# Loads that wait for the preceding TensorE operation of the order table, with the table made anew

## The chip, the cores and the metric

The kernel runs on one core of one Trainium2 chip. The metric is the device time of one launch in microseconds (us). The engines are TensorE (PE; its weight loads stand as PEld), VectorE (DVE), ScalarE (ACT), GpSimd (POOL) and SyncE (SP), whose queue issues every transfer of this kernel.

## The reference

Two independent problems, A and B, of the same shape: 16 batches of 80 rows, 32 query heads over 16 key/value heads, 512 cached keys, head width 128, all bf16. The two outputs are concatenated.

```python
def _A_ref(x, k_cache, v_cache, wq, wo):          # x (16,80,576), caches (16,16,512,128)
    q = transpose((x @ wq).reshape(B, Sq, Hq, Dh), 0, 2, 1, 3)
    k = jnp.repeat(k_cache, rep, axis=1)          # rep = 2 query heads to a key head
    v = jnp.repeat(v_cache, rep, axis=1)
    scores = jnp.einsum("bhqd,bhkd->bhqk", q, k) * (Dh ** -0.5)
    p = _softmax(scores, axis=-1)
    o = jnp.einsum("bhqk,bhkd->bhqd", p, v)
    return transpose(o, 0, 2, 1, 3).reshape(B, Sq, Hq * Dh) @ wo
...
return jnp.concatenate([a, b], axis=-1)
```

## The kernel before

The work is cut into 128 units (64 for each problem). A unit is one batch and four key heads, so 4 x 160 query rows: two heads of 80 rows share a key head. The 160 rows are handled as 128 + 32, and the four rests of 32 rows are put together to one tile of 128. So each unit has five score tiles of 128 x 512, numbered 5U to 5U+4, where 5U is the tile of the rests. For each unit and each group of eight units the operations are these; the short names are those of the code and of the text below.

- **ldk** (L631): one transposing load from the K cache for two units, so it is named by the even one (K8 is for units 8 and 9); **ldv** (L635): a plain load of V for one unit; **ldwa** and **ldwt** (L520, L524): pieces of wq; **ldwo** (L594): a quarter of wo; **ldx** and the like (L394, L450): x. K has buffers for six units, V for six.
- **xtr, xt** (L415, L433): TensorE transposes x at the start of problem A; POOL first copies a rest of x (L402).
- **qp, qt** (L551, L564): the q projection, four matmuls and one remainder per head and half; **qev** (L576 on ACT, L577 on DVE) moves q out of PSUM.
- **qk, qkr** (L678, L665): the scores; qkr does the rests of two units. **max** (L687, DVE), **exp** (L691, ACT), **rcp** (L697, DVE), **nrm** (L700, POOL) make the softmax.
- **tr** (L735): TensorE transposes the probabilities of two units, 80 small matmuls; **ptev, prev** (L752, L753, L761, L762) move them out on ACT or DVE.
- **pv** (L783): four matmuls for one key head; **oev** (L797) moves them out. Two units' pv follow their tr.
- **op** (L829): eight matmuls, half of one output tile of 128 x 288; **oea, oem, oeb** (L841, L851, L858) take it out on ACT or DVE, and **st** (L864) stores it from one of two buffers.

All operations are collected in `_Sched`. What order they run in is not worked out at run time: the string `ORDER` holds it, one letter for each operation (a stream of like operations, taken in turn), an apostrophe ahead of a letter for the other of two engines where an eviction may run on DVE or ACT, and a digit for each PSUM bank that the operation takes. `arrange` reads it. The result is one order of 5,242 operations over all engines; each engine runs its own of them in that order. `finalize` then derives the waits: an operation waits for the last writer of what it reads, and for the readers and the writer of what it overwrites, by semaphores, and leaves out a wait that an earlier one implies. A load therefore waits for nothing but the release of the buffer that it fills, and for its turn on SyncE's queue.

In the steady state a round of two units goes: tr of both, two qkr or one, then qk, pv, op and qp mixed until the next tr. The waits of PE on ACT and DVE inside a round are for banks that come free and for tiles that are moved out.

Of the kernel before, what the change touches and what calls it, by code (L numbers as in the profile page):

```python
# [8 lines left out]
AF = mybir.ActivationFunctionType  # L9
# [57 lines left out]
6425AmBh3'zg10z'yf7'xqf4f6'yf5pc2nacqc3mctc1c'uCpd2vnpc7vcm'tCb0pv'uCmwf4f3pbmvFipmvf1iCd5pmvif4d6ipmverg37w'A
Bmd0qveh5214nB'Ah0y'zf6x'yf3f2f5'zqc0acpCc4nvcd1p'uw'tc7pcmvf4tc0mcpf6b7'umCCpvpd3imvf2md0wpf5mvbpCmvd6rmveeBv
'Ag74'ABh1523qh0yn'zb6y'xqg15'zCCf7vnqbc2qwnpvf3ncpc1vmf4d0rvmpf5f6acpmd7Cpmvef4tc3mvcCpc2'Af5wumpvcd6'tf0Bd1'
uvpmieh2734AmiBih5'yzf6'xf1Cyf0v'zf2c3Cpcvc4tf7mcvpc5i'ud3vpmcwc6mtcb4Cpi'uvapmvf6f5pd1mwd2Cpmvf7bmpvmd0reeh64  # L70
75'A'BBh3'A'yg01x'zg62q'zc4'ycqc5nctc3i'ucCqnf0vf4c5qnb7tnwvpcf3pif6mbapmCf2vmb1Cpv'urmf0pd3vf5pmf4wd6Cpmvd7pm
bvmvd5rCCeevh1420A'A'BBh3z'yvwg56'xf7'yvqf4c2'zpcnc1cpf0'tif3qmc5b2unpf1mf7pcf6mCbtwpmvc5pmcd0vCipmf3avd4rmpd2
vud1mveeh3675A'B'BCh4'Avz'yg10vx'zf3J'yf2wCqc7cf6vpnc5f4pvcmb1p'tmqc7f3pmcbf2umnf6Cptc4wmcf5vd0iaCppmGd7vpmd3v
rmd2Cuveeh1546B'Aw'BCAh0v'y'zf3vb2p'xvy'zf7f4c5vmpcf0p'tf1ac3mpcc6mpbumCcwmf3Cf4pd0v'r'tc5pf2mvcd7pmvid1iumvJd
6ieeh3254A'A'BBh0y'zg16'yg23'xqb0qnqf5nbCqvnpc6vczc7'tcnf2uc4f1piGmcCpm'rvf3c6d7apf5vcmb2Cpw'utmvf1f0mpbvCpmvf
6d4mpvd1'rwd0miJeeh3652A'B'BCAh7'ywg04x'zvf1'zqf6c3'yvcqnf5c7tf2ncpc0if3'upcJmc4cab7mCppv'utmd1vpf0mf4Cbpvmpvf
5md6Cpvmd3Criwd0mveeCh7542'ABvw'ABh1y'zg06'zxvf3'yf5qf2vc7qcnvc1cnf4b0tpa'upmc7pf6mcpc1mcpd3f5mCtf2vbmpvCpmf4d
6vpmd5wCrmd7uveeh1024vA'B'ABvh6'zf7wx'yf3f5'yf0pc2ia'zcCpc6mvcf1uc4mcpc7'tcCpmf6wb2f3p'uvmpf7vd5'tpmvbiCpmivid
0mvd4'rmd6eeh7321A'B'BAh0y'zg56'xg43'zqc2qcnf1c7'ycCpb5vinCqvm'tc0ubwqnvf2rcnf1pvf6c5'tpcmf0f7pf4'uf3mb2pmCpvd
1md6wCpmpbvmCviad0rmvd5veeh3427'Aw'Ah1'BByv'zg56x'zf3'yf4qf2c7Ccqnvc1ctnf0vpc5ab7'upmpf6mbpmpcmf1f3Ctd2wmpc5vc  # L80
pCmf4id6vpmd0iFvCumd1rveeh4753Av'B'ABh2vy'zg61'xCqvf0'yf4c7'zvpcnf5f2wpc3a'tcpmc6cub7mqmc0cf4ptnf5pCbmvpmvf6d1
f2ipmiFd3Cpmvwd4rumvd5Cwveeh6702B'Av'Ah3'Byf1f5x'y'zb6'zCpvf7pmf4f2c3pmbvpmpcc0'rctmf1Cic7v'uf3apCcmd0vpmwf6c5
cmpd2vud4mvd5'teeh7163'B'BFh2'AAyFg40'z'yig57qb2'xqnqf1bnpCmc0zCwvcc6q'tf4cf1npvd0umc5vpcnf6vsb3aCpmvf4tmc2vpf
7cf1Cpmd5vpd6'uwmf4bvpmCimd7vseDiveCh4312B'A'ABvh5'yvwg76x'zf0'zqf4c1'ycqnc3f5tpf2ncc7ic'upc1amcpb6'utmpf3md0f
1Cpvmf4pvwmpbf7d5mCpKvmd3Csvd1mveeh4762'BBv'AAh5iD'yzg03K'xf7'zf4f1'yf6qCqc2vncpc5wncc0ticvmpb2DKp'umf7tpbmCmp
f4vd3pmvf5c1cmpwf0id7md6CpCsd4mvuDeveah1250A'BABvh7'yvCf3x'zf6f4v'zf1pc2'ycwpc0mcvpc7'ucp'tf3ac5mcpf0'ub2Ctmvp
mf5vbpmCd7msf1vd3mpid2vwimd0Deeh1465A'B'BAh3z'yg70'yxg24'zqc6f1cqc5nqcf3i'ub7pn'tCpvf5bmpwmqc1vcnf6td0mpc3d2sn
CCDevc'Biaf7mf4vpb5'uvCpmf2wd3'Apmf6vbpmvd0msvCeh4517vC'ABh2v'zf6x'yf0f5'yf3pvwc1a'zcpc2vmf4tcc7mpcc1'upcmb0tm
pf5Cf6'upf2vmbipwmipg14vmCd3qvmd6qvnd5nd2CCsveGeh7041B'Awv'BAh6vz'yg23'xf7'yqf5vf4'zc0qcnf6pc1nctc2icpmc3Dl0pD
mcab7pmLf5'uCuf0vmf4pbvpmd1f6Cpmvtd5mvpd0iwCsd3mwveeh2746'AAv'BCh1'Bvz'yf3f5x'zf7f2'ypf0vac6cpmc1ctc4mpcb6pmtc  # L90
3mcCpvf7'ubpmvDf1'uisf4md0pd3Cpmvd7md5wevKeh6214B'A'ABh0z'yg75'xg26'zqc1'yKqcnc4f3qic'tKc0Cnpf7wb1JnvJqubmvCpJ
nvcDf5mic2vpcf4'tb3smCpDw'uaf7mf0vpf1bvpmCf6pmd2vpd4mCsd5md7wviJeveh1360B'AvCBGh2'zAvg47x'yvf5'zqf3c6'ycqnf0c1
tf2cnpf6ac4'upcmc7tb1mppcmf4d3pmf0d5Cpvmd2uvmpf6biDwpmiCd4mvseevh6017AC'B'ABh3v'yCg25x'zwf4'yqvc1'zcpc3vncqf0v
ic6'ucl7tmDpf1nd4Lpmf2f7d5c3pmf0Cpmwetf1mvcpd6i'AvCB'uf7ad2pmvpemvh3540AmCh1yv'zf6f7CBv'xf3f5p'zf2wc4'ypcc0vmp
cc1vi'ucc6'ttcmpmud0b4pmf3Cf7mvpbpwmf5sd2vmpDd3iCmd1vaeveh4675A'B'ABh2'yg10x'zg34'yqc6'zcqnf7c2qc'tc5pinf1cb6p
mCtmvf0bpnvC'uf5wvf3maf7sqCf2d1npvc0pmb6vpmcvf5mud4Cpd3vpbmvFmwDd2siCeFevh5607A'B'BDCAvh4'zyg12'xyf5'zvwf3qc0c
vpc6nctf4i'uf7pc1macpb6mpmf0qf3bmpnCd5twmf7f1vc4Cppmcd2vpmd0vumd3svDeeh4176B'A'ABh2z'yg05'xCCvf1'z'yqf4c7vpcnf
3c2wpmcf6apvb0muvqf1mbpnd3mCpf4tc2vmpf5f7wcpmc1icvCsd6'tpmDvd4Cumd0veveh7251A'BAvh3'yzCvf6'yf4Bf2v'xb7pwpmf3c0
pamcbpmzf6mc4spc'tc2Cuf5cmvc0pf7'tcvd6Cp'uimvf3d2ipmwDid4id0mveeh3157B'ABh2y'zg60'xAg13'yqf4'zb5pnqf7mbpnqf6mf
4Cf2Csac0vncpc7vf5'tqCcmc1vpb0nvpmcvpf6bf3mtCwmupvid1mCwc4cd2pvmd5vid7'u'rCveeh4360B'B'AAwvh2'zg15vx'yf7'zqvf3  # L100
c6'ycqnf0c4pcnf2uc1ac'tpb5mpmf7tbpmpmf1c3Ccpmvf6f4d2Cpmvid7pmFvd0imwd1ruCveeh6453B'Av'BAh2y'zvg17'yxf6'zf4qc5f
2qcnf0c3pancb1p'umf7c3CpmtpbvmvCpf6f4mcvpc5mwricd2pmFvf7d1Cpmiwd0umvd6tCeveh7543A'B'BwAh2'zvf6x'yf1f5v'zf0pc4'
yf7pcmc3pcc2mictd6u'tmf1CCpf2vc3cpmvf5ib4p'uavmpbvmpCd3mvd0wm'rd1veeh4725A'B'ABh6z'yg30'xzg17'yqf2c5qcnf6b4p't
nCpvf3f5mqbvampc0ncc2CpC'ucc6'rc'twvvf0mud1pmf2f4b3qvmpwDinbCpivmf0vrd5mCpd6vd3mveevh2740A'B'BCAh1v'yzg53'xwzf
6'yb2vqqnf7c4pcnc5pmcf0tf3ic1'upcamf4tbmppf6mc1f5Cpd0mvf7Cpmcvd4pmwd3uimd6vrevGeh5127BC'A'Bh4vz'yg06'xvCAf5'yq
c1vc'zqc3wnf4cf7v'tiuc2nf0pf1af3pb6mpmcpc5mcCpf4wbmpvmuf7d0vmCpJd5vpmd3ivrmd1teeh7264A'B'ABCh5wv'zyf0'xf1pf3'y
# [37 lines left out]
class _Sched:  # L144
# [9 lines left out]
    def add(self, eng, key, emit, reads=(), writes=(), dsem=None, name="", stream=None, alloc=(), alt=None, hard=(), parts=()):  # L154
        op = _Op()
# [57 lines left out]
    def finalize(self):  # L213
# [7 lines left out]
        for op in ops:  # L221
            deps = {}
# [720 lines left out]
```

## Time and profile before

| | |
|---|---|
| median of 3 runs | 721.21 us (721.03 to 723.38) |
| profiled execution, its own time | 723.83 us |
| its span, first to last instruction | 722.1 us |
| granted TensorE clock, mean | 0.998 |
| PE, ACT, DVE, POOL busy | 98%, 90%, 85%, 60% |
| moved by DMA | 160.72 MB, mean 223 GB/s |

Shares of busy time are of the span. PE's matmuls are pipelined and their ends are modelled, so "busy" says that PE had work, not that it ran at its peak. "Idle before" is time in which an engine had nothing to do, put down to what ended the wait; "issue" is idle time with no wait that the profile shows. A load's line on SyncE is the time that its queue is held, and the landing is counted from the issue.

### The profile page before, as it was taken

How to read it: one execution, taken by the hardware profiler on the slowest of the kernel's cores; microseconds unless marked ns; L12 is line 12 of the kernel's file. 1: busy time of each engine (PE TensorE's matmuls, PEld its weight loads, DVE VectorE, ACT ScalarE, POOL GpSimd, SP SyncE). 2: the span in 40 equal slices, each digit the busy share in tenths (PEclk: the TensorE clock that was granted, in tenths of full speed). 3: DMA queues.
4: the chain of work that ended last, by engine and by line, in shares of the span. 5: the costliest groups of instructions: out<-in, count | busy, mean ns of one | idle time of the engine just before them, and what ended most of it. 6: DMA issues, size and time to landing. Idle time of an engine off the chain costs nothing.

```text
span 722.1 us, 26076 instructions
## 1 busy us (share of the span) xinstructions
PE 705.6 (98%) x10820; PEld 512.0 (71%) x10820; DVE 614.7 (85%) x1341; ACT 648.7 (90%) x1770; POOL 432.0 (60%) x650
## 2 busy tenths in 40 slices
PE   7898999999999999999999999899999999999998
PEld 4565677777777767767677777677777777777777
DVE  2997989889788888888989888698898988889994
ACT  2998989999999999989999999799999999999893
POOL 0566656666666564755766576455665656566663
PEclk9999999999999999999999999999999999999999
DMA  9999997999879999999999899789799889979390
GB/s 238 247 271 264 269 254 178 245 254 238 218 195 231 268 220 226 262 226 229 258 226 238 229 211 267 180 212 217 149 296 231 209 230 222 254 178 211 101 225 23
DMA packets 374166, 160.72 MB, mean 223 GB/s; under 512 B 278560, under 2 KB 370976, under 8 KB 374048
## 3 DMA queue, kind: packets, MB, share of 16 engines
q1 hardware_dynamic: 374048, 159.05, 92.2%
q8 instruction: 86, 1.41, 0.8%
q14 instruction: 32, 0.26, 0.1%
HBM read 87.65 MB, written 2.95 MB: 125 GB/s over the span
## 4 chain that ended last, share of the span: by engine, by line
PE 90%; SPq 4%; DVE 3%; DMA 1%; issue 1%; ACT 0%
PE ps L829 22%; PE ps L783 19%; PE ps L551 17%; PE ps L678 15%; PE ps L735 11%; PE ps L665 4%; PE ps L564 3%; SPq L631 2%; DVE negmax L687 2%; DMA v_sb<-in_A_v_cache_dram 1%; SPq L520 1%; DMA out_dram<-osb 1%; SPq L394 0%; SPq L524 0%; ACT p_sb L691 0%
## 5 line engine op out<-in xcount | busy, mean ns | idle before, releaser
L700 POOL TENSOR_SCALAR p_sb<-p_sb,rinv 128x512 bf16<-128x512 bf16 x640 | 430.2, 692 | 272.6 <-DVE rinv L697 272.2
L691 ACT ACTIVATE p_sb<-ps,negmax 128x512 bf16<-128x512 f32 x640 | 438.0, 711 | 19.1 <-DVE negmax L687 16.9
L687 DVE TENSOR_REDUCE negmax<-ps 128x1 f32<-128x512 f32 x640 | 410.1, 678 | 20.7 <-PE ps L678 12.3
L783 PE MATMUL ps<-pT,v_sb 128*128 128x160 bf16 x2048 | 181.5, 233 | 2.8 <-issue 2.2
L829 PE MATMUL ps<-wo_sb,oT 128*128 128x288 bf16 x1280 | 181.6, 287 | 2.2 <-issue 2.2
L783 PEld LDWEIGHTS ps<-pT,v_sb 128*128 128x128 bf16 x2048 | 152.7, 98 | 42.3 <-ACT pT L752 5.2
L678 PE MATMUL ps<-kT,qT 128*128 128x512 bf16 x512 | 166.4, 381 | 2.6 <-DVE rinv L697 1.1
L551 PE MATMUL ps<-xT,wq_sb 128*128 128x320 bf16 x1024 | 163.5, 299 | 0.9 <-DMA wq_sb<-in_A_wq_dram 0.6
L829 PEld LDWEIGHTS ps<-wo_sb,oT 128*128 128x128 bf16 x1280 | 123.4, 98 | 44.5 <-issue 2.9
L691 ACT ACTIVATION_READ_ACCUMULATOR p_sb<-ps,negmax 128x1 f32 x640 | 145.1, 227 | 0.0
L551 PEld LDWEIGHTS ps<-xT,wq_sb 128*128 128x128 bf16 x1024 | 97.5, 98 | 43.8 <-issue 1.3
L752 ACT COPY pT<-ps 128x512 f32<-128x512 f32 x194 | 105.0, 603 | 8.7 <-PE ps L735 6.7
L577 DVE TENSOR_SCALAR qT<-ps 128x320 bf16<-128x320 f32 x125 | 57.0, 483 | 41.9 <-PE ps L564 41.7
L735 PEld LDWEIGHTS ps<-ident,p_sb 64*128 64x128 bf16 x5120 | 82.6, 95 | 9.6 <-ACT p_sb L691 1.7
L735 PE MATMUL ps<-ident,p_sb 64*128 64x64 bf16 x5120 | 86.1, 190 | 0.9 <-ACT qT L576 0.3
L576 ACT ACTIVATE qT<-ps 128x320 bf16<-128x320 f32 x131 | 50.9, 437 | 28.5 <-PE ps L564 27.8
L797 DVE CAST oT<-ps 128x320 bf16<-128x320 f32 x138 | 65.6, 479 | 9.0 <-PE ps L783 8.6
L678 PEld LDWEIGHTS ps<-kT,qT 128*128 128x128 bf16 x512 | 45.4, 98 | 31.7 <-DVE pT L753 4.4
L797 ACT CAST oT<-ps 128x320 bf16<-128x320 f32 x118 | 51.7, 444 | 9.9 <-PE ps L783 9.1
L753 DVE COPY pT<-ps 128x1024 bf16<-128x1024 bf16 x62 | 42.0, 682 | 3.7 <-PE ps L735 3.6
L697 DVE RECIPROCAL rinv<-rowsum 128x3 f32<-128x3 f32 (+1 forms) x256 | 39.6, 159 | 5.4 <-ACT p_sb L691 4.6
L665 PE MATMUL ps<-kT,qT 128*32 128x512 bf16 x512 | 37.4, 383 | 1.3 <-issue 1.3
(31 smaller groups left out, 147.7 us busy)
## 6 DMA issues: line engine op xcount, KB each, us to landing
v_sb<-in_A_v_cache_dram SPq DMA_DIRECT2D x64, 512.0 KB, 5.0
v_sb<-in_B_v_cache_dram SPq DMA_DIRECT2D x64, 512.0 KB, 5.2
wo_sb<-in_A_wo_dram SPq DMA_DIRECT2D x8, 576.0 KB, 6.5
wo_sb<-in_B_wo_dram SPq DMA_DIRECT2D x8, 576.0 KB, 6.2
wq_sb<-in_B_wq_dram SPq DMA_DIRECT2D x4, 1024.0 KB, 6.9
out_dram<-osb SPq DMA_DIRECT2D x40, 72.0 KB, 3.9
wq_sb<-in_A_wq_dram SPq DMA_DIRECT2D x8, 256.0 KB, 4.4
wq_sb<-in_A_wq_dram SPq DMA_DIRECT2D x2, 1024.0 KB, 7.1
```

What stands on the lines that cost most here:

```text
L551: last = e.matmul(ps[:, vbq[h].phys, QO:QO + 320], lhsT=wq_sb[:, wsl, ck, hi * 128:(hi + 1) * 128], rhs=xT[:, half, ck, n0:n0 + 320], star ...
L577: return e.tensor_scalar(dst, src, SCALE, None, op0=AluOpType.mult)
L665: last = e.matmul(ps[32 * g4:32 * g4 + 32, vb_.phys, :], lhsT=qT[:, qsl_, bl_, g4 * 160 + 128:g4 * 160 + 160], rhs=k_of(U_, g4), start=Tru ...
L678: return e.matmul(ps[:, vb.phys, :], lhsT=qT[:, qsl, bl, gl * 160:gl * 160 + 128], rhs=k_of(U, gl), start=True, stop=True)
L687: return e.tensor_reduce(negmax[:, si:si + 1], ps[:, vb.phys, :], axis=AX.X, op=AluOpType.max, negate=True)
L691: return e.activation(p_sb[:, psl, :], ps[:, vb.phys, :], AF.Exp, bias=negmax[:, si:si + 1], scale=1.0, accum_out=rowsum[:, ss, k:k + 1])
L700: return e.tensor_scalar(p_sb[:, psl, :], p_sb[:, psl, :], rinv[:, ss, k:k + 1], 1.0, op0=AluOpType.mult, op1=AluOpType.mult)
L735: last = e.matmul(dst, lhsT=p_sb[64 * h:64 * h + 64, psl2[i_][k_], j * 128:(j + 1) * 128], rhs=ident[64 * h:64 * h + 64, 64 * h:64 * h + 6 ...
L752: return e.copy(dst.bitcast(F32), ps[:, vb.phys, :].rearrange("p (j n) -> p j n", j=4))
L783: last = e.matmul(ps[:, vo.phys, off:off + 160], lhsT=v_sb[:, vs, gl, j * 128:(j + 1) * 128], rhs=pT[:, pts, j, :, 32 * gl:32 * gl + 32], ...
L797: return (e.copy if en == "act" else e.tensor_copy)(dst, src)
L829: last = e.matmul(ps[:, vb.phys, 0:DC], lhsT=oT[:, sp_ * (HH // 2) + i, rb * 128:(rb + 1) * 128], rhs=wo_sb[:, 2 * c3 + sp_, i, :], start= ...
```

## The change

In `finalize`, operations are gone through in the table's order. The last TensorE operation seen is remembered, and each operation whose name begins with "ld" (all 248 loads, not the 40 stores) gets it as a further dependency. So a load is issued no earlier than the end of the TensorE operation that stands ahead of it in the table. Waits implied by an earlier one on the same queue are left out as before: of SyncE's operations 186 now carry a wait for PE, 140 did before.

```diff
 class _Op:
     __slots__ = ("eng", "key", "seq", "emit", "reads", "writes", "dsem", "stream", "alloc", "alt",
-                 "deps", "signals", "sidx", "waits", "clock", "name", "hard", "parts")
+                 "deps", "signals", "sidx", "waits", "clock", "name", "hard", "parts", "paced")
...
         op.parts = list(parts)
+        op.paced = name.startswith("ld")
...
         cur_ver = {}
+        last_pe = None
         for op in ops:
...
             for d in op.hard:
                 deps[id(d)] = d
+            if op.eng == "pe":
+                last_pe = op
+            elif op.paced and last_pe is not None:
+                deps[id(last_pe)] = last_pe
...
 ORDER = """
-oEHoj7KHKHIIHNk6Hk0NMl1Hk4LMIMEIl5d6ad3k4k0eL'BMMd4Ad1d3eId7B'AId0d2aed5'A'Bd4d1eA'Bd3e'ABe'AK'BKf0f3ipf6f1af5
...
+HKIHHHIKIoEj2oNNHHIk6ak4k0l5EMLMMd1d0d2el7d3Iek4d6I'Bd5ALBMed4Kd0aKied3'A'B'B'Ad7k2d1ed5eMBA'A'A'Bf0pg3iaf5f4d
...
```

The table is new from its first letter to its last. What differs once it is decoded:

- PE has the same 1,842 operations. The round's frame (tr, qkr, qk, pv, op and qp of the same numbers between two tr) is the same; inside a round neighbours change places.
- Four evictions move from ACT to DVE (1,129 operations become 1,125, and 1,337 become 1,341). Which of the evictions run where, and their places, change throughout.
- SyncE's first loads. Before: wq 0.0, x 0.0, wt 0.0, x 0.1, wt 0.1, wq 1.0, wt 1.0, wq 0.1, 0.2, 0.3, wt 1.1, wq 1.1, K0, wq 1.2, 1.3, K2, x 1.0, x 1.1, V0, K4, V1, V2, K6, V3. After: wq 0.0, x 0.0, wq 1.0, wt 0.0, wt 0.1, wq 0.1, wt 1.0, x 0.1, wt 1.1, wq 0.2 (waits for the warm-up matmuls), wq 0.3, wq 1.1, K0 (xtr0), wq 1.2 (qp0.1.1), wq 1.3, x 1.0 (qp0.3.0), K2 (qp0.3.1), x 1.1, V0, V1 (qkr0), K4, V2 (qk6), V3 (tr1), K6.
- From there on nearly every load stands behind a later PE operation than the release of its buffer. Two examples, as PE's order runs from the operation waited for to the first reader. K8: qk33, then pv3.2 pv3.3 tr4 qk34 tr5 qkr7 qk36 op pv4.0 pv4.1 qk37 qk38 pv4.2 pv4.3 qp1.6.0 pv5.0 qk39 pv5.1 pv5.2 op pv5.3, then qk41. V127: pv125.2, then pv125.3 op op tr126 tr127 op pv126.0 to pv126.3, then pv127.0.

More of the change, by code (lines that the diff above doesn't have):

```diff
@@ L67 @@
[L67 to L106, printed above, removed]
@@ L128 @@
+c2cf7c3cf6c5cf0bc4tppCpsm'umf7if3cig62pqpCqm'u'tmnDb1bf0vvvvwvwvvvh4675mnh3'zpsCyf2'zf1f6f4b5pxmymCppmc7cDc0cc
+3cbm'tuCpmc0ic'utsCb6vwvvvvwvvvbh0271h5b3'xsyz'zyc0cDc6cc1Dcc5bt'tuscb7'ubb3sDDbsD
 """
```

88 lines of the change are left out of this document (63 added, 25 removed).

## The prediction

> **What bounds the kernel now.** I read the page first: busy shares, then the chain that ended last.
>
> ```profile
> PE 705.6 (98%) x10820; PEld 512.0 (71%) x10820; DVE 614.7 (85%) x1341; ACT 648.7 (90%) x1770; POOL 432.0 (60%) x650
> PE 90%; SPq 4%; DVE 3%; DMA 1%; issue 1%; ACT 0%
> ```
>
> TensorE is busy 98% of the span and is 90% of the chain, so a change that leaves its matmuls as they are can save at most the rest, 722.1 - 705.6 = 16.5 us. Where that rest lies is in the windows by stage (busy time of each engine, granted clock, DMA share, GB/s):
>
> ```profile
> 0.00:40.00 40.00, 33.98 (x348) 19.35 (x350) 25.85 (x60) 25.68 (x70) 15.33 (x30) 1.00 1.06 243
> 40.00:100.00 60.00, 56.29 (x917) 39.69 (x909) 52.92 (x113) 54.46 (x149) 36.32 (x55) 1.00 1.15 262
> 100.00:300.00 200.00, 199.24 (x3072) 146.23 (x3070) 173.17 (x375) 188.65 (x520) 124.19 (x185) 1.00 0.97 230
> 450.00:458.00 8.00, 5.79 (x128) 3.88 (x126) 5.17 (x10) 7.22 (x20) 3.96 (x6) 1.00 0.77 187
> 458.00:461.40 3.40, 3.40 (x15) 1.89 (x14) 1.43 (x4) 0.34 (x2) 1.26 (x2) 0.50 0.09 20
> 600.00:722.00 122.00, 119.53 (x1868) 90.03 (x1864) 102.69 (x223) 104.19 (x284) 71.80 (x107) 1.00 0.70 168
> ```
>
> PE idles 6.0 us in the first 40 us, 3.7 us in the next 60, 0.8 us in the 200 after that, 2.2 us in the 8 us from 450, and 2.5 us in the last 122, most of it the end. From 458.0 to 461.4 the granted clock was 0.50, straight after the stop at 455, which costs half of 3.4, 1.7 us, without being idle. So the game is in the start and in a few single stops; the middle runs without gaps. PE's waits say who ends them (total, times, longest):
>
> ```profile
> PE ps L829 <- issue: 2.2, 1, 2.2
> PE ps L783 <- issue: 2.2, 4, 1.4
> PE ps L415 <- DMA acc<-in_A_x_dram: 1.3, 2, 0.7
> PE ps L665 <- issue: 1.3, 1, 1.3
> PE ps L433 <- POOL acc L402: 0.6, 1, 0.6
> PE ps L783 <- DMA v_sb<-in_A_v_cache_dram: 0.6, 1, 0.6
> PE ps L551 <- DMA wq_sb<-in_A_wq_dram: 0.6, 1, 0.6
> ```
>
> Two kinds. Waits for a load come to 1.3 + 0.6 + 0.6, and the 0.6 for POOL's copy of x is one more, all in the first 40 us. The others, "issue", ended without any semaphore; the three long ones are 1.4, 1.3 and 2.2 us. The timeline shows two of them, one inside a run of equal matmuls, where the order of instructions asks for no wait:
>
> ```profile
> 53.02 0.85 PE L783 MATMUL ps<-pT,v_sb 128*128 128x160 bf16 x10
> 55.25 0.30 PE L783 MATMUL ps<-pT,v_sb 128*128 128x160 bf16 x2 [1.37 <-issue]
> 457.47 1.35 PE L829 MATMUL ps<-wo_sb,oT 128*128 128x288 bf16 x7 [2.21 <-issue]
> ```
>
> **What a load costs, and what the new wait does to it.** SyncE's line of loads (duration on its queue, ns) and the time from issue to landing, first for K (L631), then for V (L635):
>
> ```profile
> L631 SPq DMA_TRANSPOSE kT<-in_A_k_cache_dram x32: 3894/5556/9213, 8.6 to 331.3; - x32
> DMA to landing us min/median/max: 6.1/8.1/12.9
> DMA to landing us min/median/max: 3.8/5.0/9.4
> ```
>
> A K load holds SyncE's queue for 5.6 us and lands 8.1 us after its issue; a V load lands after 5.0 us. Everything behind a waiting load on that queue waits too: later loads, and the output stores. In exchange the queue is now idle where it used to run ahead as far as free buffers allowed.
>
> The unit costs of PE's operations, to turn an order into time, stand in the chain (start, us, what):
>
> ```profile
> 59.17 1.09 PE ps L551 x8
> 81.18 0.98 PE ps L829 x8
> 95.56 1.17 PE ps L735 x80
> 152.71 1.11 PE ps L783 x16
> 236.03 1.02 PE ps L665 x16
> 314.51 1.19 PE ps L678 x5
> ```
>
> So one qp is 1.09/2 = 0.55, one op 0.98, the transposes of a pair 1.17, one pv 1.11/4 = 0.28, one qkr of two units 0.51, one qk 0.24 us. The lead of a load is PE's work between the end of the operation that it now waits for and the first operation that reads it. For K8 (wait for qk33, read by qk41) that is 10 pv, a pair of transposes, one qkr, 5 qk, 2 op and one qp: 2.8 + 1.2 + 0.5 + 1.2 + 2.0 + 0.55 = 8.2 us. Counted so for all 64 K loads, the median lead falls from 19 us (from the last wait that the old order gave) to 14, and the shortest, beyond the first two loads, are 8.2, 8.4, 8.8, 9.2, 9.4, 9.4, 9.9, 10.3 and 10.3 us. For the 128 V loads the median falls from 30 to 17 us; five lie below 7: 5.6, 6.0, 6.0, 6.1 and 6.8 (V127, the first of these: 5 pv, 3 op and a pair of transposes, 1.4 + 2.9 + 1.2).
>
> **Term 1, the start: -1.7 us.** The first loads change places. Timeline of before:
>
> ```profile
> 1.24 3.27 PE L367 MATMUL ps<-wo_sb 128*128 128x512 bf16 x8 [1.24 <-DVE wo_sb L360]
> 2.60 0.60 SPq L394 DMA_DIRECT2D acc<-in_A_x_dram  x1
> 5.17 1.71 SPq L520 DMA_DIRECT2D wq_sb<-in_A_wq_dram  x3
> 9.63 1.79 PE L551 MATMUL ps<-xT,wq_sb 128*128 128x320 bf16 x12 [0.56 <-DMA wq_sb<-in_A_wq_dram]
> 15.30 4.86 SPq L631 DMA_TRANSPOSE kT<-in_A_k_cache_dram  x1
> 20.21 2.06 SPq L394 DMA_DIRECT2D acc<-in_A_x_dram  x2
> 22.82 6.90 SPq L631 DMA_TRANSPOSE kT<-in_A_k_cache_dram  x1
> 24.98 0.38 PE L415 MATMUL ps<-ident,acc 128*128 128x128 bf16 x4 [0.61 <-DMA acc<-in_A_x_dram]
> 25.20 0.59 PE L678 MATMUL ps<-kT,qT 128*128 128x512 bf16 x2
> ```
>
> ```profile
> acc<-in_A_x_dram SPq DMA_DIRECT2D x2, 288.0 KB, 3.8
> ```
>
> The second half of x (part 1.0) stood behind K2 and made PE wait 0.61 us at 24.98; it now goes ahead of it, and the wait is gone. V1 stood behind K4 and cost 0.6; it now goes ahead of it, gone. In the first 10 us wq piece 0.1 moves from 8th to 6th place, which lifts the 0.56 at 9.63, while x part 0.1 moves from 4th to 8th: issued at 5.2 instead of 2.6, it lands 3.8 later, near 9 us, and its wait (0.6 before) stays about what it was. The new waits cost nothing here: the 10th load waits for the warm-up matmuls, over at 1.24 + 3.27 = 4.5 us, when SyncE has issued only about six. Together -0.6 - 0.6 - 0.5. What is late next: K2 is issued half a microsecond later, 15.8, lands near 15.8 + 8.1 = 23.9, and is needed at 25.20 less what was gained; so at most 1.3 us of the gain gets past that point at once. Bounds: 0 (all is taken by the next wait) and -2.5 (the 0.6 for POOL goes too).
>
> **Term 2, the stops without a semaphore: -1.3 us.** Stops of 1.4 and 1.3 us fall in the stage of the highest DMA share (1.15), where the old queue ran furthest ahead. In the new order that stage's loads are spread: K8 waits for qk33, K10 for qk42. I take one of the two as gone, as an estimate from that coincidence only; bounds 0 and -2.7, and a new stop elsewhere (+2.2, with the half clock +3.9) can't be excluded. [...]
>
> **Term 3, loads that come late: +0.6 us.** Leads of 8.2 and 8.4 us meet a K landing after 8.1: a few tenths each for K8 and K10, nothing for the rest. The cover is PE's own work between; where a K takes longer than its lead, PE stands for the difference, since nothing else may pass in its queue. Bounds: 0 with K at its minimum of 6.1, and with K at 10.5 (half way from median to maximum) the shortfalls of the nine leads above sum to 2.3 + 2.1 + 1.7 + 1.3 + 1.1 + 1.1 + 0.6 + 0.2 + 0.2 = 10.6 us. V at 5.0 is covered everywhere; at 7 us the five short ones would cost 4.5.
>
> **Parts at nothing.**
>
> ```profile
> L797 ACT CAST oT<-ps 128x320 bf16<-128x320 f32 x118 | 51.7, 444 | 9.9 <-PE ps L783 9.1
> ```
>
> The matmuls are the same in number and shape, and nearly the same in order. Four evictions move from ScalarE (94% busy in 100 to 300 us) to VectorE (87%), 4 x 0.44 = 1.8 us of work off the fuller engine, hidden behind PE on either. PE's additional signals for SyncE are part of matmuls that run anyway. Each output store keeps over 5 us of PE work between its latest wait and the eviction that needs its buffer. Bounds of the remade middle are under the second rival.
>
> **Sum.** The profiled execution took 723.8 us, span 722.1; the runs' median, 721.2, is 2.6 lower. The stop at 455 with its half clock is 2.2 + 1.7 = 3.9, so I take 2.6 of it as this execution's own. 723.8 - 2.6 - 1.7 - 1.3 + 0.6 = **718.8 us**. A measurement of this kernel tells about 0.3%, 2.2 us, from no change: "faster" is below 719.0, "slower" above 723.4.
>
> **Rivals.** (a) *Late K loads decide.* The new wait replaces a free-running queue by leads of 8 to 10 us. It decides once a paced K needs over 9.4 us from its wait to its landing. For it: landings up to 12.9 us. Against: the long ones come with a backlog, and pacing removes backlog. Price: the 10.6 us above instead of 0.6, 728.8. Chance 0.17.
> (b) *The remade middle is looser.* 64 rounds of two units, each with its orders on ScalarE and VectorE changed; a tenth of a microsecond lost per round is 6.4 us, 725.2. For it: ScalarE is 94% busy there, so an eviction placed a little late has little to hide in. Against: the order differs by neighbours, and the old one lost 0.8 us in 200. Chance 0.14.
> (c) *Loads were never on PE's path after the start, and the stops stay.* Term 2 falls out: 720.1, no measurable change; the same if terms 1 and 3 cancel. [...] Chance 0.24.
> (d) *Both early stops, and further small waits, go*: the calmer DMA also lets VectorE and ScalarE start on time in 40 to 100 us, where PE idles 3.7 us. 718.8 less 1.3 and less 2.5 of those: 715. Chance 0.10.
> Forecast: 0.35, spread 717 to 721, so some of it falls in the band.
>
> **How the numbers follow.** Faster: 0.10 from (d), 0.28 of the forecast, 0.04 of (c): 0.42. Slower: (a) and (b), 0.31. Same: the rest, 0.27. The range reaches from 713.5 (a little below (d)) to 728.8, the price of (a), which leaves out less than 2 in 10. The likeliest case's own range is 716 to 722.
>
> **What would show it.** Right: no wait of L415 for x at about 24 us and none of L783 for V1; PE idle in 0 to 100 us near 7 instead of 9.7 us; at most one stop of over 1 us without a releaser before 100 us; PE over 99% busy in 100 to 300 us; median K landing below 8.1. Wrong by (a): PE waiting for kT at L678 or L665, at qk41, qk51, qkr111. Wrong by (b): waits for DVE or ACT spread evenly over the middle, with VectorE waiting for PE more than before.

## The result, and the profile after

The changed kernel takes 717.62 us (median of 8 runs, 715.94 to 721.89), the kernel before beside it 721.59 us (8 runs, 721.03 to 724.85): a ratio of 0.9944, 95% interval 0.9919 to 0.9970. (Ratios leave disturbed runs out, so they are not exactly the quotients of the medians.) The profiled execution took 720.19 us with a span of 718.3, 3.8 us below the 722.1 of before. Lines are 6 higher than before: qk is L684, pv L789, op L835, qp L557, qkr L671, ldk L637, ldv L641.

The page's busy shares and the chain by engine:

```profile
PE 704.7 (98%) x10820; PEld 511.7 (71%) x10820; DVE 617.8 (86%) x1345; ACT 647.4 (90%) x1766; POOL 431.9 (60%) x650
PE 89%; DMA 7%; DVE 1%; SPq 1%; issue 1%; ACT 0%; POOL 0%
```

PE's idle time fell from 16.5 to 718.3 - 704.7 = 13.6 us. DMA, 1% of the old chain, is 7% of the new one: loads are now issued late enough to be followed back into. The windows by stage, after (start:end, length, then busy us of PE, PEld, DVE, ACT and POOL with their counts, granted clock, DMA share, GB/s):

```profile
0.00:40.00 40.00, 33.48 (x326) 19.05 (x326) 24.96 (x58) 25.05 (x67) 14.20 (x29) 1.00 1.04 235
40.00:100.00 60.00, 59.32 (x949) 41.65 (x950) 55.60 (x120) 57.39 (x160) 39.32 (x59) 1.00 1.10 257
100.00:300.00 200.00, 198.86 (x3073) 145.47 (x3073) 174.00 (x377) 187.26 (x512) 123.09 (x183) 1.00 0.99 228
300.00:450.00 150.00, 148.17 (x2322) 108.36 (x2315) 132.49 (x292) 139.10 (x379) 93.41 (x140) 1.00 0.99 228
450.00:600.00 150.00, 149.69 (x2343) 109.97 (x2341) 130.87 (x285) 140.26 (x384) 91.28 (x136) 1.00 0.97 229
600.00:718.30 118.30, 115.14 (x1826) 87.17 (x1825) 99.87 (x219) 98.33 (x268) 70.61 (x105) 1.00 0.76 185
```

and the two stages of before that the prediction did not show:

```profile
300.00:450.00 150.00, 149.03 (x2333) 108.97 (x2331) 134.02 (x297) 139.42 (x381) 92.93 (x140) 1.00 0.97 238
450.00:600.00 150.00, 147.52 (x2308) 107.74 (x2305) 126.08 (x276) 136.30 (x372) 91.46 (x137) 0.99 0.91 220
```

PE's idle time, stage by stage, before and after: 6.0 and 6.5; 3.7 and 0.7; 0.8 and 1.1; 1.0 and 1.8; 2.5 and 0.3; 2.6 and 3.2 (from 600 to the end of the span). Two stages gained, 3.0 and 2.2 us, and the second of them also lost its half clock (1.7 us of busy time). The other four lost 0.5, 0.4, 0.9 and 0.6 us, 2.3 in all (from unrounded rows). The two that gained are those that held the long stops without a semaphore. (The trace of the changed kernel holds no clock records, so its 1.00 are no readings; that PE had no half clock there is told from its matmuls: after the first 4 us and apart from the stops, five output matmuls in a row start at most 125 ns apart (122 in the median; 240 in the half clock of before), five of the projections at most 175 (136 in the median). The second profile of this kernel, below, has records, and they say 1.00 from 5.4 us on.) Of PE's waits after (total, times, longest):

```profile
PE ps L557 <- issue: 1.3, 2, 0.8
PE ps L557 <- DVE xT L426: 1.1, 1, 1.1
PE ps L684 <- DMA kT<-in_A_k_cache_dram: 1.0, 1, 1.0
PE ps L789 <- issue: 1.0, 1, 1.0
PE ps L421 <- DMA acc<-in_A_x_dram: 0.7, 2, 0.5
PE ps L671 <- DVE rinv L703: 0.6, 1, 0.6
PE ps L671 <- DMA kT<-in_B_k_cache_dram: 0.3, 1, 0.3
PE ps L671 <- DMA kT<-in_A_k_cache_dram: 0.2, 1, 0.2
```

The wait for V1 is gone, and the one for x at 25 us nearly. A K wait of 1.0 us stands in their place, and two more waits of the start are new: 1.1 us for VectorE's copy of x, ahead of the first projections (now at 7.05 instead of 9.63 us), and 0.6 us for rcp at 22.96. The timeline shows the K wait at K2's first reader:

```profile
26.49 0.59 PE L684 MATMUL ps<-kT,qT 128*128 128x512 bf16 x2 [1.04 <-DMA kT<-in_A_k_cache_dram]
```

K2 was issued at 16.59 and landed at 26.35, 9.8 us later; in the kernel before it was issued at 15.30 and landed 8.3 us later. Over all K loads the landing (min/median/max) is not shorter than the 6.1/8.1/12.9 of before:

```profile
DMA to landing us min/median/max: 6.1/8.7/12.7
```

### The profile page after: what moved, and what is told of

Read it like the earlier page. It is cut to its first block, busy times and chain, and to the rows that moved or that the text cites. A ratio compares the mean times of both kernels' runs of the same rounds, so it can differ in the third digit from the quotient of the medians.

```text
span 718.3 us, 26080 instructions
## 1 busy us (share of the span) xinstructions
PE 704.7 (98%) x10820; PEld 511.7 (71%) x10820; DVE 617.8 (86%) x1345; ACT 647.4 (90%) x1766; POOL 431.9 (60%) x650
## 4 chain that ended last, share of the span: by engine, by line
PE 89%; DMA 7%; DVE 1%; SPq 1%; issue 1%; ACT 0%; POOL 0%
PE ps L835 21%; PE ps L789 18%; PE ps L557 18%; PE ps L684 15%; PE ps L741 10%; PE ps L671 4%; PE ps L570 3%; DMA kT<-in_A_k_cache_dram 3%; DMA kT<-in_B_k_cache_dram 2%; DVE negmax L693 1%; DMA xst<-in_B_x_dram 1%; DMA acc<-in_A_x_dram 1%; DMA wq_sb<-in_A_wq_dram 1%; DMA out_dram<-osb 1%; ACT p_sb L697 0%
## 5 line engine op out<-in xcount | busy, mean ns | idle before, releaser
L789 PE MATMUL ps<-pT,v_sb 128*128 128x160 bf16 x2048 | 182.1, 233 | 1.0 <-issue 1.0
L789 PEld LDWEIGHTS ps<-pT,v_sb 128*128 128x128 bf16 x2048 | 152.8, 98 | 37.9 <-DVE pT L768 4.9
L835 PE MATMUL ps<-wo_sb,oT 128*128 128x288 bf16 x1280 | 179.8, 286 | 0.0
L684 PE MATMUL ps<-kT,qT 128*128 128x512 bf16 x512 | 167.5, 380 | 2.4 <-DMA kT<-in_A_k_cache_dram 1.0
L557 PE MATMUL ps<-xT,wq_sb 128*128 128x320 bf16 x1024 | 165.4, 299 | 2.8 <-issue 1.3
L835 PEld LDWEIGHTS ps<-wo_sb,oT 128*128 128x128 bf16 x1280 | 123.2, 98 | 40.8 <-ACT pT L758 0.6
L557 PEld LDWEIGHTS ps<-xT,wq_sb 128*128 128x128 bf16 x1024 | 97.9, 98 | 46.8 <-issue 2.5
L758 ACT COPY pT<-ps 128x512 f32<-128x512 f32 x190 | 103.4, 603 | 7.1 <-PE ps L741 5.2
L583 DVE TENSOR_SCALAR qT<-ps 128x320 bf16<-128x320 f32 x124 | 56.5, 484 | 37.5 <-PE ps L570 37.4
L684 PEld LDWEIGHTS ps<-kT,qT 128*128 128x128 bf16 x512 | 45.1, 97 | 31.8 <-ACT pT L758 8.3
L803 ACT CAST oT<-ps 128x320 bf16<-128x320 f32 x116 | 50.0, 442 | 5.0 <-PE ps L789 4.6
L759 DVE COPY pT<-ps 128x1024 bf16<-128x1024 bf16 x66 | 44.4, 683 | 4.7 <-PE ps L741 4.6
L671 PE MATMUL ps<-kT,qT 128*32 128x512 bf16 x512 | 37.6, 383 | 1.5 <-DVE rinv L703 0.6
```

The source lines that it names most:

```text
L557: last = e.matmul(ps[:, vbq[h].phys, QO:QO + 320], lhsT=wq_sb[:, wsl, ck, hi * 128:(hi + 1) * 128], rhs=xT[:, half, ck, n0:n0 + 320], star ...
L583: return e.tensor_scalar(dst, src, SCALE, None, op0=AluOpType.mult)
L671: last = e.matmul(ps[32 * g4:32 * g4 + 32, vb_.phys, :], lhsT=qT[:, qsl_, bl_, g4 * 160 + 128:g4 * 160 + 160], rhs=k_of(U_, g4), start=Tru ...
L684: return e.matmul(ps[:, vb.phys, :], lhsT=qT[:, qsl, bl, gl * 160:gl * 160 + 128], rhs=k_of(U, gl), start=True, stop=True)
L758: return e.copy(dst.bitcast(F32), ps[:, vb.phys, :].rearrange("p (j n) -> p j n", j=4))
L789: last = e.matmul(ps[:, vo.phys, off:off + 160], lhsT=v_sb[:, vs, gl, j * 128:(j + 1) * 128], rhs=pT[:, pts, j, :, 32 * gl:32 * gl + 32], ...
```

## A count that explains the stops

The stops without a semaphore have a place in common that no view names, but that the views can count. The page of before says:

```profile
q8 instruction: 86, 1.41, 0.8%
```

Queue q8 brought 86 packets of instructions, 1.41 MB, each of 16,384 bytes in the trace. PE's stream has 10,820 matmuls, as many weight loads and 340 semaphore and drain instructions in the trace: 21,980, or 256 for each packet. Read by this count, the queue brought PE's instructions in blocks of 256, one for every 126 matmuls or so, on average every 705.6 / 86 = 8.2 us of PE's busy time. The windows from 0 to the end of the four long stops of before count the matmuls ahead of it (the bracket behind PE's time):

```profile
0.00:55.24 55.24, 47.85 (x595) 29.25 (x596) 39.78 (x89) 40.66 (x111) 24.69 (x44) 1.00 1.08 255
0.00:63.27 63.27, 54.60 (x721) 33.89 (x721) 45.88 (x102) 47.36 (x128) 28.79 (x50) 1.00 1.09 250
0.00:90.93 90.93, 81.20 (x1098) 52.26 (x1099) 70.44 (x154) 72.47 (x199) 45.66 (x76) 1.00 1.11 258
0.00:457.46 457.46, 443.79 (x6771) 317.68 (x6772) 391.13 (x852) 414.89 (x1134) 272.26 (x413) 1.00 1.00 238
```

With weight loads and semaphore instructions these are instructions 1216, 1473, 2240 and 13,760 of the stream: 192, 193, 192 and 192 beyond a multiple of 256. (The count starts at the first instruction of the profile; what PE ran ahead of it is not counted. The place 192 to 194 is called a block boundary from here on.) The stop at 90.9 is put down to DVE by the waits, but sits at the same place. And the stop at 55.25, which began at 53.88, has a packet of q8 right ahead of it (DMA queues, 52.8 to 54.0 us):

```profile
q8 instruction: 1, 0.02, 5.4%
```

In the trace that packet ran from 52.85 to 53.89, and PE went on 1.36 us after its end. For the other three the pause from the packet's end to PE's restart is 1.23, 1.63 and 1.28 us. This suggests a theory that the first four runs were not chosen for: these stops are PE waiting for a block of its own instructions that comes late (theory F below).

## The experiments

The experiments ran on three chips, four to a chip, each time with the kernel before beside them: there its medians were 723.49, 723.21 and 723.46 us, and on the last chip its 33 executions ranged from 717.04 to 727.91 us. The ratios are to these.

**First four: which half of the change does it?** Three theories were on record: P, the wait gives the gain; T, the new table gives it; M, the calmer middle pays.

Table only:

```diff
-            elif op.paced and last_pe is not None:
+            elif False and op.paced and last_pe is not None:
```

> The new table without the new wait. Theory P (the wait gives the gain: with the queue held back, PE's stops without a semaphore between 40 and 100 us do not happen): the two stops of over 1 us come back, about 720 to 721.5, ratio to before 0.997 to 1.000. Rival T (the new table gives the gain, by the order of the first loads and of the evictions): as the changed kernel, 717.6, ratio 0.994, no stop of over 1 us before 100 us.

Measured: 721.11 us, ratio 0.9973 (0.9948 to 0.9998). The early stops are gone without the wait, which is against P; but others stand at 217 us (0.8 us, at matmul 3115, where the changed kernel stopped too), 258, 513 and 521 us. The last is put down to ACT, but it too sits at a block boundary:

```profile
PE ps L789 <- ACT p_sb L697: 1.3, 1, 1.3
PE ps L557 <- issue: 1.2, 2, 0.9
PE ps L789 <- issue: 1.1, 2, 0.8
PE ps L671 <- issue: 0.8, 1, 0.8
```

Wait only, that is the changed code with the old string:

```diff
 ORDER = """
-... (the new table)
+... (the old table)
 """
```

> The old table with the new wait. Theory P: the stops before 100 us go, 718 to 719, ratio about 0.996; no wait for kT, since the old table's loads stand early in it. Rival T: the old time, 721.6, or slower by late loads.

Measured: 731.83 us, ratio 1.0106 (1.0068 to 1.0143). PE's waits:

```profile
PE ps L421 <- DMA acc<-in_A_x_dram: 3.4, 1, 3.4
PE ps L835 <- issue: 2.8, 1, 2.8
PE ps L557 <- DVE osb L864: 2.2, 1, 2.2
PE ps L557 <- DMA wq_sb<-in_B_wq_dram: 1.0, 1, 1.0
PE ps L671 <- issue: 1.0, 1, 1.0
```

The first x load stands behind the warm-up matmuls in the old table, so now it waits for them, and PE starts on x at 8.3 instead of 5.2 us; the projections behind this wait ran at half pace (the first eight in 2.34 us, 1.25 at full pace). A store that stands behind a paced load in SyncE's queue is late and costs 2.2 us, a late wq piece 1.0. Stops came back at matmuls 721, 1098 and 6771 of before (1.0, 0.8 and 2.8 us), at other times and with the queue held back. So P's account of them falls: neither a queue that runs ahead nor its absence decides.

Wait in the first 103 us alone, and wait in the rest alone, both with the new table:

```diff
-            elif op.paced and last_pe is not None:
+            elif op.paced and last_pe is not None and op.key < 714:     # the start
+            elif op.paced and last_pe is not None and op.key >= 714:    # the other kernel: the rest
```

> The new table, loads wait for PE only up to about 103 us, later ones only for their buffers. Theory P: as the changed kernel within a microsecond, 717 to 718.5, since the stops lie in the start. Rival T: 717.6 too; a third, M (the calmer DMA of the middle pays): 720 or more.

Measured: 720.73 us, ratio 0.9958 (0.9931 to 0.9986).

> The new table, loads wait for PE only from about 103 us on. Theory P: as without the wait, 720 to 721.5, with stops in 40 to 100 us. Rival T: 717.6. M: 718 or less.

Measured: 717.31 us, ratio 0.9903 (0.9872 to 0.9934). By these numbers M seemed to hold: pacing the middle worth some 4 us on top of the table. But the profiles differ in PE's stops at block boundaries: counting those of 0.3 us or more, 4.1 us in all in the table-only kernel, 2.8 with the start paced, 1.1 with the rest paced. The next runs test whether that is all.

**The changed kernel again, on another chip.**

> The changed kernel unaltered, so that the next ones have it on the same chip. Theory F (a PE stop that no wait explains is PE waiting for its own instructions: a block of 256 instructions comes in as one 16 KB packet of the instruction queue, and the packet is late) expects the ratio to stay near 0.994 and, in the profiled run, zero to two stops of 0.7 us or more after 40 us, every one of them at PE instruction 192 to 194 of a block of 256, not necessarily at the places of the first profile of this kernel. Rival R (a stop belongs to a place in the program: to what the operation there does or reads) expects the stop at the same operation again, the third output matmul of the 36th V unit at 219 us, 1.0 us.

Measured: 717.90 us, ratio 0.9915 (0.9885 to 0.9946). Its stops came at matmuls 2611 (0.8 us), 7651 (0.4) and 7778 (1.0), all at 192 to 194 of a block, while the first profile of the same kernel had them at 1099, 3115 and 4627. A further 0.7 at matmul 5137 is a wait for x's transposes in problem B, which the waits name and which has no packet near it; so "every one" in the expectation of F was too much, and R's stop at 219 us did not come. Two of the first profile's three, 0.5 and 0.8 us there, came back at 0.2 us each (1099 and 4627). So the length of a stop changed from one execution to the other; where in the block PE stopped, at 192 to 194, did not.

**The kernel before, shifted by 30 instructions.**

```diff
-            for _ in range(NWARM):
+            for _ in range(5):
                 last = e.matmul(ps[:, vw.phys, :], lhsT=ones, rhs=warm, start=True, stop=True)
+            for _ in range(18):
+                last = e.matmul(ps[:, vw.phys, 0:64], lhsT=ones, rhs=warm[:, 0, 0:64], start=True, stop=True)
```

> The kernel before with 23 warm-up matmuls in place of 8 (5 of 512 columns and 18 of 64, together a little shorter), which shifts everything later in PE's instruction stream by 30 instructions and leaves table, loads and waits as they were. The kernel before had stops at matmuls 595, 721, 1098 and 6771 counted from the first (instructions 1216, 1473, 2240 and 13760), and the run with the old table and the wait had them again at 721, 1098 and 6771. F expects those that come back at the same counts, which are now operations 15 matmuls earlier in the program, or none at all where a block boundary now lies in a slower stretch; none at the old operations, which now stand at matmuls 610, 736, 1113 and 6786. R expects them at the old operations, so at matmuls 610, 736, 1113 and 6786. Time: F and R both within 3 us of the kernel before (718.5 to 724.5); F alone allows a difference from which blocks are late.

Measured: 718.06 us, ratio 0.9920 (0.9887 to 0.9953). The old table without any new wait, with 15 more warm-up matmuls, gains as much as the whole change. Its windows:

```profile
0.00:40.00 40.00, 35.61 (x359) 21.11 (x361) 25.67 (x60) 25.15 (x70) 14.94 (x30) 1.00 1.09 236
40.00:100.00 60.00, 59.21 (x944) 41.90 (x940) 55.60 (x120) 57.08 (x159) 39.83 (x60) 1.00 1.13 266
100.00:300.00 200.00, 200.00 (x3150) 146.67 (x3149) 173.22 (x376) 189.51 (x521) 125.47 (x187) 1.00 1.02 237
300.00:450.00 150.00, 147.19 (x2236) 108.13 (x2233) 130.85 (x290) 136.85 (x374) 90.77 (x136) 0.99 1.01 231
450.00:600.00 150.00, 149.98 (x2351) 110.46 (x2349) 131.35 (x287) 140.70 (x384) 92.82 (x138) 1.00 0.95 223
```

From 40 to 100 us PE idles 0.8 us instead of 3.7, and 450 to 600 is full. Matmul by matmul against the kernel before: at 34.8 us the two are level to 0.02 us, so the warm-up's new form gave nothing; the shifted one is ahead by 1.4 us at the old place of the stop at 55, by 1.9 at that at 63, 3.2 at that at 91, 3.7 at a shorter one at 220, falls back by 3.1 at its own one long stop and the half clock behind it, and gains 4.1 over the old stop and half clock of 457. At the end it is 5.2 ahead. The time is 0.4 us below what either theory had room for. The old first stop lay inside this run of pv, which now has none (timeline):

```profile
53.15 0.99 PE L785 MATMUL ps<-pT,v_sb 128*128 128x160 bf16 x12
...
347.58 1.09 PE L785 MATMUL ps<-pT,v_sb 128*128 128x160 bf16 x7 [2.32 <-issue]
```

The one at 347.58 stands ahead of matmul 5133, instruction 10,432, again 192 of a block. The wait-only kernel, and the old table with the wait on the rest (two runs further down), have stops of 1.5 and 1.7 us ahead of matmul 5133 too (the kernel before one of 0.4), there a matmul of qp, here one of pv 15 matmuls earlier in the program. A count shared by three kernels, at two different operations: windows from 0 of the wait-only kernel, of the old table with the rest paced, and of this one,

```profile
0.00:355.66 355.66, 343.80 (x5133) 243.97 (x5133) 298.14 (x647) 316.54 (x867) 207.62 (x315) 1.00 1.01 236
```

```profile
0.00:354.02 354.02, 341.30 (x5133) 242.43 (x5133) 297.81 (x647) 316.73 (x867) 207.67 (x315) 1.00 1.04 237
```

```profile
0.00:347.57 347.57, 339.60 (x5133) 242.52 (x5134) 295.52 (x643) 315.68 (x866) 207.61 (x315) 1.00 1.05 240
```

F's places hold and R's do not: nothing stopped at matmuls 610, 736, 1113 or 6786. The only other stop over 0.7 us after 40 us, 0.8 at 56.5, is a K load that came late, which the waits name.

**A quarter of the V traffic.** The changed kernel, which from unit 6 on reads one of the four key heads of each V load and leaves out the other three, so that its output is not the reference's.

```diff
-            def em_ldv(e, vc_ap=vc_ap, b=b, q=q, vs=vs):
-                src = vc_ap[b, 4 * q:4 * q + 4, :, :].rearrange("g (p j) d -> p g (j d)", j=4)
-                return e.dma_start(v_sb[:, vs, :, :], src)
+            def em_ldv(e, vc_ap=vc_ap, b=b, q=q, vs=vs, ng=4 if U < 6 else 1):
+                src = vc_ap[b, 4 * q:4 * q + ng, :, :].rearrange("g (p j) d -> p g (j d)", j=4)
+                return e.dma_start(v_sb[:, vs, 0:ng, :], src)
```

> The changed kernel, but from the seventh V load on only one of the four key heads of each is read, 128 KB instead of 512, so the output isn't the reference's. All instructions of PE, VectorE and ScalarE stay. It takes nearly all V traffic, some 42% of the loaded bytes after the start, off the DMA engines. If the instruction packets are late because they share the DMA engines with the loads (theory F1), they start sooner after a block boundary than the median of 2.3 to 2.9 us that the profiles so far show, below 1.8 us, no stop of 0.7 us is left after 40 us and K's landing falls below 8 us; the time goes to 713 to 716. If they are late for another reason (F2: the request itself is made late, or the queue is served late), the delay stays above 2.2 us, stops of the old kind stay, and only the K waits of 0.2 to 1.0 us go: 715.5 to 718.

Measured: 717.02 us, ratio 0.9915 (0.9888 to 0.9941), the changed kernel's own ratio on this chip; span of the profiled run 714.8. K's landing:

```profile
DMA to landing us min/median/max: 6.1/7.6/10.9
```

PE's stops by the waits:

```profile
PE ps L789 <- issue: 1.7, 2, 1.1
```

The median delay from PE's passing a block boundary to the start of the next packet, counted in the trace, fell from 2.58 to 1.77 us, as F1 expected, but two stops stayed, 1.1 and 0.7 us, both at block boundaries, and the time is F2's. So the load on the DMA engines seems to be part of a packet's lateness (one profile), not all of it, and taking V's traffic away is worth no time that these runs can tell.

**Old table, the wait on the rest alone.** The wait-only kernel with `and op.key >= 715` behind the condition.

> The old table with the wait for all loads but the first 100 us or so of the table's (from place 715 on): it leaves out the start, where the old table's first x load stood behind the warm-up matmuls and cost 3.4 us when it was paced. Theory S (the old table with the wait was slow for its start alone, and pacing the middle is worth 2 to 4 us with either table, as the step from table alone to table with the wait from 103 us on suggests) expects 717 to 720. Rival N (the wait is good only with a table that was made for it: in the old one the places of the loads were free of any consequence, and loads and stores that stand late in it now become late) expects 723 to 728, with new stops after 300 us on loads of wq or on a store held up behind a paced load, as the run with the old table and the full wait had at 533 and 646 us (1.0 and 2.2 us).

Measured: 725.77 us, ratio 1.0028 (0.9997 to 1.0060): N, not S. The start's 3.4 us are gone, and other loads of the old order are late, with the store at 641 us again:

```profile
PE ps L421 <- DMA acc<-in_A_x_dram: 3.3, 2, 2.9
PE ps L557 <- DVE osb L864: 2.0, 1, 2.0
PE ps L671 <- issue: 1.8, 1, 1.8
```

The longest part of the first, 2.9 us at 27.25, is in the stretch that was not paced, and N had not named it. The x load there stands behind K0 and K2, which held SyncE's queue for 6.8 and 6.7 us (5.5 and 4.9 in the kernel before), so it was issued at 23.1 instead of 20.2 us; why the two K loads took longer, no run shows. The two stops at block boundaries over 1 us, 1.8 at 66 and 1.7 at 354, are at old counts, 721 and 5133.

**The same shift for the new table, with and without the wait.** The diff is the one above.

> The changed kernel (new table, wait for all loads) with the same shift of PE's instruction stream by 30 as in the shifted kernel before. That one took 0.992 of the kernel before with the old table and no wait, as much as the change itself. Theory L (the time that separates these kernels is which instruction blocks are late for PE; the wait itself is worth nothing) expects this one anywhere from 715 to 721, without order against the changed kernel, and its stops of 0.7 us or more after 40 us at PE instruction 192 to 194 of a block, not at the operations at which the changed kernel had them (matmuls 3115, 2611, 5137 and 7778, which are now 3130, 2626, 5152 and 7793). Theory W (the wait is worth 2 to 4 us by a calmer queue whatever the alignment, and the shifted kernel before had luck) expects 2 us or more below the table-only kernel with the same shift, and no stop over 1.2 us.

> The new table without the wait, shifted by 30 as well. Without the shift it took 0.9973 of the kernel before and had stops of 0.8, 0.9 and 1.3 us at 258, 513 and 521 us. L expects these at other operations or gone, and a time within 1.5 us of the shifted changed kernel, to either side: 715 to 721. W expects it 2 to 4 us above the shifted changed kernel, 720 to 723.

Measured: with the wait 719.64 us, ratio 0.9946 (0.9921 to 0.9971); without it 718.73 us, ratio 0.9928 (0.9906 to 0.9949). That is L: shifted, the table alone is not 2 us slower than the table with the wait, but if anything 1 us faster. With the wait there is a stop of 1.65 us, where W allowed none over 1.2. Both, and the last kernel below, stop ahead of the same matmul, 2107, instruction 4288, 192 of a block (windows from 0, with the wait, then without):

```profile
0.00:152.33 152.33, 146.19 (x2107) 100.36 (x2108) 125.45 (x274) 130.66 (x360) 85.24 (x135) 1.00 1.04 237
```

```profile
0.00:149.91 149.91, 143.77 (x2107) 99.74 (x2108) 125.33 (x274) 130.38 (x360) 84.88 (x134) 1.00 1.09 251
```

In the profiled executions 1.6 us of the 2.4 between these two times arose before 18 us, where the first q projections ran at half pace in one of the two, without a gap between them, so no load held them; no clock record of that profile covers them (last section), so what slowed them is not shown (timeline; with the wait, then without):

```profile
8.09 3.38 PE L559 MATMUL ps<-xT,wq_sb 128*128 128x320 bf16 x12 [1.11 <-DVE xT L428]
```

```profile
7.92 1.80 PE L559 MATMUL ps<-xT,wq_sb 128*128 128x320 bf16 x12 [1.11 <-DVE xT L428]
```

**The kernel before, shifted by 128.** 72 small warm-up matmuls in place of the 8.

> The kernel before with 72 small warm-up matmuls in place of the 8, a shift of 128 instructions, half a block; the warm-up ends about 0.6 us later, just before the first x is used. If instruction blocks make the stops, none is left at the old operations (now matmuls 659, 785, 1162 and 6835) and those that there are sit at 192 to 194 of a block. L expects 715 to 724, drawn anew: if it is below 720 again, the old alignment was a bad one; at 722 or more, the shift by 30 was a good one. If the shift by 30 won by anything else than the stops (the warm-up's form), this one should win by it too and keep its stops of the old kernel.

Measured: 722.80 us, ratio 0.9996 (0.9970 to 1.0023). No stop at the old operations, but new ones: 0.9 us at matmul 470, 1.6 at 1477, 0.9 at 8033 and 1.6 at 9546, instructions 960, 3008, 16,320 and 19,393, all at 192 or 193 of a block. So a shift is not a cure; the shift by 30 was a good draw.

**Wait on the rest, shifted by 30.** The candidate to beat both kernels.

> The new table with the wait only from 103 us on, the fastest of the kernels so far by its ratio (0.9903), with the shift by 30: a version that could beat both kernels. L expects 715 to 721, again without order. W expects it with the shifted changed kernel or up to 1 us below it, 715 to 718, since the first K loads go out early and the rest is paced.

Measured: 718.29 us, ratio 0.9940 (0.9912 to 0.9969). It does not beat the changed kernel, and the 0.9903 of the same version without the shift is likely no more than one draw either. Not every long stop is a block's: here PE also stood for 1.3 us at 640 us, off the boundary, until ScalarE's copies of the probabilities were done.

All ratios to the kernel before, by version and shift of PE's stream:

| | no shift | by 30 | by 128 |
|---|---|---|---|
| old table, no wait | 1 | 0.9920 | 0.9996 |
| new table, no wait | 0.9973 | 0.9928 | |
| new table, wait (the change) | 0.9944 and 0.9915 | 0.9946 | |
| new table, wait on the start | 0.9958 | | |
| new table, wait on the rest | 0.9903 | 0.9940 | |
| old table, wait; wait on the rest | 1.0106; 1.0028 | | |

A shift that changes no order, no load and no wait moves the old kernel by 0.8%; among the versions with the new table the whole spread is 0.7%. The shift's other warm-up is not quite without effect of its own: by the matmuls' pace, two of the three shifted kernels with the new table (those with a wait) still ran at half pace from 8 to 11 us in their profiles (12 and 11 matmuls in those 3 us, 24 in the third). The wait takes part in no ordering that survives the shift. If the new table itself is worth a little (its eight ratios run from 0.9903 to 0.9973, the three of the old from 0.992 to 1), it is by at most a few tenths of a per cent, and these runs do not settle it.

## Why the prediction was right in number and wrong in its steps

The time, 717.62 against 718.8, lies in the range and on the likeliest side. The sum came out by luck: two terms missed in opposite directions.

- **Term 1, the start: -1.7.** The failed step is "What is late next: K2 ... at most 1.3 us of the gain gets past that point at once". x's wait at 25 us and V1's went as described, but K2 was ready at 26.4, not 23.9 (issued 0.8 us later than forecast and 1.7 longer on its way), PE stood 1.04 us for it, and the waits of 1.1 and 0.6 us for VectorE, which the term did not have, came with the new order of the start. Idle time in the first 40 us rose from 6.0 to 6.5. The term came out at +0.5, outside its bounds of 0 and -2.5. An 8.1 us median landing was applied to a load that is issued among those of x and wq; the maximum of 12.9 was the number to bound it by.
- **Term 2, stops without a semaphore: -1.3.** Mis-sized and misread. Both early stops went, and so did the third at 91 us (PE idle in 40 to 100 us: 3.7 to 0.7, that is -3.0 instead of -1.3; rival (d) had that far more nearly). But "one of the two ... from that coincidence", the highest DMA share, was the wrong cause: the table-only kernel lost them with the queue free, the wait-only kernel kept two of the three with the queue held, and the old kernel lost them by 15 warm-up matmuls. The forecast had no term for instructions that come late; what the runs show are stops of 0.3 to 2.8 us at the boundaries of blocks of 256, with the packet's end 1.2 to 2.2 us ahead of the restart.
- **Term 3, late loads: +0.6.** Right in size and wrong in place: after the start, K waits of 0.3 and 0.2 us, at 583 and 191 us by the timeline, none at the readers of K8 and K10. The leads were counted rightly: 8.3 and 8.7 us from issue to first read (8.2 and 8.4 forecast); K8 landed in 6.7 us, K10 in 8.6, just in time. Rival (a) at 10.6 us did not come, though the reason given against it, "pacing removes backlog", was wrong: the median landing rose from 8.1 to 8.7 us.
- **Parts at nothing and rival (b).** In 100 to 300 us PE is 99.4% busy (99.6% before), as forecast; from 300 to 450 it lost 0.9 us, most of it the stop of 0.8 at 317.9, which is a block boundary again. No tenth was lost in each round.
- **Sum.** It took 2.6 us off as the profiled execution's own part in the stop at 455. That stop did go, with its half clock. But it is no accident of one execution: the wait-only kernel has a stop at the same matmul, 2.8 us, and a shift of the old stream by 30 or 128 takes it away. Half clock came back too: in 42 of the 88 executions of the kernel before beside the experiments the mean granted clock was below 1.00, and in 3 of the 19 of the changed kernel; where in those executions it fell is not on record.

Put together for the two profiled executions: stops at block boundaries (of 0.3 us or more) fell from 6.7 to 2.3 us and the half clock behind one of them, 1.7 us, went: -6.1. The span fell by 3.8. So all else got 2.3 us longer, 0.5 of it idle time in the start. Taken without its block stops, the changed kernel is not faster than the one before. With the spans of the other profiles the same subtraction gives about 713 to 714 us for the old table at all three shifts, 713 to 714 for the new table without the wait, 715 to 716 with it, and 714 to 717 with it on the rest (with the half pace of their start taken off as well, the two shifted ones with a wait come to 713.5 and 715); each is one execution, so this is a hint and no proof. Shown are the places of the stops and that a shift alone can give the whole gain. That nothing of the 0.6% is owed to the change's purpose is what the runs make likely, not what they prove.

What stays open is why a packet is late. Its delay behind PE's passing a boundary is 2.3 to 3.1 us in the median of every full-traffic kernel, 1.8 with a quarter of the V bytes, and 3.2 to 7.4 at the stops. How fast PE uses up a block may count as well: a block takes it 7.7 to 8.2 us in the median, and ahead of most stops less than that (at those of before 5.4 to 6.6, once 8.4); a stretch of small transposes (80 in 1.17 us) uses it up sooner than one of projections (8 in 1.09 us). No run varied either alone.

## What to carry to other kernels

Before a change below 1% is credited, run a control that keeps the program and shifts the instruction stream of the bounding engine (a few more small matmuls at the start); here it moved the time as much as the change did. When PE stops with no releaser, or with one that is named for only some of the stops, count its instructions up to the stop: the equal remainders by 256 here, 192 to 194 at stops of different operations, spoke for late instructions and against late data. A wait that paces loads must come with an order made for it: on the old order it cost 1%, through one load behind the warm-up and one store behind a paced load. Bound a load that is issued among others by the longest landing (12.9 us here), not the median (8.1): K2 took 9.8.

## What the runs showed of the hardware that was not expected

- PE's instructions came in 16 KB packets, by the count 256 to a packet (86 packets for 21,980 instructions in the kernel before), and in each profile PE stopped one to six times, 0.3 to 2.8 us each (shorter ones left out), at the same offset in a block, 192 to 194. That it stood for the late packet is the reading that the shifts fit (packet's end 1.2 to 2.2 us ahead of the restart); no view names it as what PE waited for. The two profiles of the changed kernel share two of these places, one at 0.5 and 0.2 us, the other at 0.8 and 0.2.
- A stop cost more than itself in the kernel before: behind the one of 2.2 us came 1.7 us of half clock. Five times while PE had work the clock column of these profiles shows half clock, for about 3.4 us each time: at 458 us in the kernel before, at 347 in the shifted one, at 28 and 643 in the old table with the rest paced (mean clock 0.96 from 0 to 40 us, 0.99 from 600 to 714), at 8 in the kernel with a quarter of V. Ahead of three of them the views show how long PE idled: 2.2 of the 3.0 us from 455 in the kernel before, the 2.3 us of the stop up to 347.6 in the shifted one, 1.9 of the 3.4 us from 4.3 with a quarter of V. A long stop did not always bring it: behind the one of 2.8 us in the wait-only kernel 42 matmuls start in the 4 us from 462, where the half clock of before has 15 in 3.4, and the column says 1.00. What decides between the two is not shown. The windows show such a stretch of the shifted kernel, then the one of the kernel with a quarter of V, with the idle window ahead of it:

```profile
347.57:350.00 2.43, 2.42 (x16) 1.90 (x16) 0.74 (x2) 0.00 (x0) 0.00 (x0) 0.50 1.04 248
4.28:7.70 3.42, 1.54 (x19) 1.02 (x18) 1.50 (x5) 0.00 (x0) 0.34 (x1) 1.00 1.08 279
7.70:11.10 3.40, 3.40 (x15) 1.58 (x14) 0.00 (x0) 0.00 (x0) 0.29 (x1) 0.50 0.99 258
```

- In the shifted kernel with the wait the twelve projections at 8 us took 3.38 us instead of 1.80, half pace, while the clock column says 1.00:

```profile
8.00:11.00 3.00, 2.91 (x12) 1.64 (x12) 0.03 (x1) 0.00 (x0) 0.29 (x1) 1.00 1.11 276
```

  That 1.00 is no reading: this trace has no clock record before 12.84 us, and the column prints 1.00 where there is none. The matmuls came to full pace just there. In the other profiles that have such records the first begins at 4.0 to 17.0 us. Ahead of the one at 4.0, in the kernel before, the eight warm-up matmuls took 3.27 us, 0.41 each, where a score matmul of the same width later takes 0.24; so at the start the pace of the matmuls is what to read.
